# Building the operands of a feed-forward half inside attention instead of beside the output projection

## The chip, the cores and the metric

The kernel runs on one core of a Trainium2 chip. Its engines work side by side, each through its own instruction queue in order: TensorE (PE, matrix products and transposes, results in PSUM), VectorE (DVE), ScalarE (ACT), GpSimd (POOL) and SyncE (SP, which here only issues transfers). ACT also issues some transfers. The metric is device time in microseconds (us) of one execution; lower is better.

## The reference

One transformer block on 2048 tokens of width 576: a modulated layer norm, attention with 32 heads of 18 over four segments of 512 tokens with a running memory, an output projection with a gated residual, a second modulated layer norm, and a gated feed-forward network of width 4608 with its own gated residual.

```python
h = _layernorm(x) * (1 + ca) + sa
x = x + ga * _A_ref(h, A_wq, A_wk, A_wv, A_wo, A_beta)   # per segment: softmax + memory; then @ wo
h = _layernorm(x) * (1 + cb) + sb
x = x + gb * ((_silu(h @ w_gate) * (h @ w_up)) @ w_down)
```

All is float32. The kernel reaches that precision with products of split operands: a tile is rounded to a "high" part (a cast on ACT), and the rest, the "low" part, is formed by a subtraction on DVE; high x high, high x low and low x high are added in PSUM.

## The kernel before

**Attention** runs in 33 turns `u` of 11 steps `k`. Unit `u` is segment `s = u // 8` and group of four heads `q = u % 8`. In each step PE gets products of unit `u` (`p2_step`), the row maxima of unit `u + 2` (`p1_seq`) and events from a hand-written table `PAT`: the product with the values (`V`), its copy and transposes (`E`, `c`, `d`), the output projection of an earlier segment (`R`, `S`, `T`, `M`, `X`) and its layer norm, which stores the normalised tokens to DRAM (`xhD`). The event `n` stores a unit's row maxima to DRAM from ACT (`mD<-mr`, L211), and SP loads them back (`load_m`, `qs<-mD`, L174) for the first matmul of the next unit. At the start of each unit SP loads the stacks of a later one (`ks`, `qs`). Segment `s` is projected during the units of segment `s + 1`, so the last segment's projection stands alone behind attention.

**The feed-forward network** is done in two halves `t` of 1024 tokens. Each product of four blocks is formed by seven products of sums of blocks (a Strassen scheme). So each half needs seven operands `y[:, o]`, built from four blocks of normalised tokens, transposed and scaled: `h00`, `h10`, `h01`, `h11` (first index: which 512 tokens; second: which half of the columns). Operand 0 is `h00`, 1 is `h01`, 2 is `h11`, 3 is `tb = h10 - h00`, 4 is `tc = h11 - tb`, 5 is `cu = h11 - h10`, 6 is `h01 - tc`. Each comes in three column blocks `kb` (two of 128, one of 32 + 64 rows in which both parts stand together). The weights go through the same scheme: `load_o` loads a block of weights `O`, four `sum_o` on POOL add up its sums (L1091), `prep_r` and `prep_w` split them.

In the second half the operands are built during the first half (`prep2`), stored to DRAM (`yD`) and loaded (`load_y`). In the first half they are built by `t_prep` after attention, interleaved by the lists `TT` and `EE` with the last segment's projection (the seam): loads of `xhD` (L909, L912), transposes on PE (L918), scaling on ACT or DVE (L925, L922), differences on POOL and DVE (L946, L949, L953, L959), and 21 pairs of a cast (L932, L934) and a subtraction (L938, L940).

The projection itself: `wo_r` transposes, `wo_s` and `wo_t` split, `wo_m` issues the 14 matmuls of a block (L707; eight blocks, two PSUM banks), and `wo_x` (L712, DVE) adds the residual and so frees the bank. Work appended to `later` is issued on DVE at the next `flush`.

After the seam the loop over pairs of weight columns starts, 14 steps each; beside its products a pair issues `load_d`, `mul_d`, `sum_d` and `prep_d` for the second matrix (`dr`, L1108 to L1126). In the first pair the products with the second matrix (`pd`, L1257) are not there yet. The order on every engine is the order of the program.

Of the kernel before, what the change touches and what calls it, by code (L numbers as in the profile page):

```python
# [7 lines left out]
F32 = mybir.dt.float32  # L8
# [7 lines left out]
P = 128  # L16
# [29 lines left out]
T0 = 2  # L46
E0 = 4
EV = ((0, 0, 1), (0, 1, 0), (2, 1, 1))
EH = "aaap"
# [8 lines left out]
WC = 4  # L58
NE = 2
# [15 lines left out]
def block(ctx: ExitStack, tc: tile.TileContext, x, wqk, wv, wo, beta, wgu, wd, c, w_mod, out):  # L75
# [70 lines left out]
    yD = [dr.tile([P, 5, L], F32, tag=f"yD{o}", name=f"yD{o}") for o in range(7)]  # L146
# [511 lines left out]
    op = pool(p2r, "op", side="right")  # L658
    woh = w3.tile([P, 5, D], F32R, tag="woh", name="woh")
# [15 lines left out]

    def wo_r(s, i):
# [6 lines left out]
        xr = o3.tile([P, D], F32, tag="xr", name="xr")  # L683
        oT[s, i] = (oh, ol, xr)
        r = L * s + P * i
        nc.sync.dma_start(xr, x[r:r + P, :])
# [213 lines left out]
    def t_prep():  # L900
        xs, h = {}, {}

        def load(kb, kh):
            xt = xs[kb, kh] = xp.tile([P, 8, P], F32, tag="xs", name="xs")
            c0 = 288 * kh + 128 * kb
            for b in range(2):
                src = xhD[b][:, :, c0:c0 + min(P, 288 - 128 * kb)]
                if kb < 2:
                    nc.sync.dma_start(xt[:, 4 * b:4 * b + 4, :], src)  # L909
                else:  # L910
                    for j in range(3):
                        nc.sync.dma_start(xt[:, 4 * b:4 * b + 4, 32 * j:32 * j + 32], src)  # L912

        def trans(kb, kh, b):
            n = P if kb < 2 else 96
            pt = ps.tile([P, 4, P], F32, tag="t", name="pt", bufs=4)
            for i in range(4):
                nc.tensor.transpose(pt[:n, i, :], xs[kb, kh][:, 4 * b + i, :n], ident)  # L918
            h[kb, b, kh] = f = (hx if kb == 1 else tp).tile([P, L], F32, tag="sg", name="h", bufs=4 if kb == 1 else NSG)
            c = 3 * kh + kb  # L920
            if (kb, kh, b) in EV:
                nc.vector.tensor_scalar(f[:n], pt[:n].rearrange("p a b -> p (a b)"), colm[:n, c, 0:1], colm[:n, c, 1:2],  # L922
                                        op0=ALU.mult, op1=ALU.add)
            else:
                nc.scalar.activation(f[:n], pt[:n].rearrange("p a b -> p (a b)"), AF.Identity,  # L925
                                     scale=colm[:n, c, 0:1], bias=colm[:n, c, 1:2])

        def hi(kb, o, f, eng):
            n = P if kb < 2 else 96
            d = y[:n, o, kb if kb < 2 else 4]  # L930
            if eng == "a":
                nc.scalar.copy(d, f[:n])  # L932
            else:
                nc.gpsimd.tensor_scalar(d, f[:n], 1.0, 0.0, op0=ALU.mult, op1=ALU.add)  # L934

        def lo(kb, o, f):
            if kb < 2:
                nc.vector.tensor_tensor(y[:, o, 2 + kb], f, f32(y[:, o, kb]), op=ALU.subtract)  # L938
            else:
                nc.vector.tensor_tensor(y[64:96, o, 4], f[64:96], f32(y[64:96, o, 4]), op=ALU.subtract)  # L940

        def ew(kb):
            n = P if kb < 2 else 96
            t1, t2, t3, t4 = [tp.tile([P, L], F32, tag=g, name=g, bufs=2 if g == "cu" else 1) for g in ("tb", "tc", "cu", "cu")]
            h00, h10, h01, h11 = [h[kb, b, kh] for kh in range(2) for b in range(2)]
            nc.gpsimd.tensor_tensor(t1[:n], h10[:n], h00[:n], op=ALU.subtract)  # L946
            hi(kb, 0, h00, "a")
            yield
            nc.vector.tensor_tensor(t3[:n], h11[:n], h10[:n], op=ALU.subtract)  # L949
            lo(kb, 0, h00)  # L950
            hi(kb, 1, h01, "a")
            yield
            nc.gpsimd.tensor_tensor(t2[:n], h11[:n], t1[:n], op=ALU.subtract)  # L953
            lo(kb, 1, h01)
            hi(kb, 2, h11, "a")
            yield
            lo(kb, 2, h11)
            hi(kb, 5, t3, EH[0])
            nc.gpsimd.tensor_tensor(t4[:n], h01[:n], t2[:n], op=ALU.subtract)  # L959
            yield  # L960
            hi(kb, 3, t1, EH[1])
            lo(kb, 5, t3)
            yield
            hi(kb, 4, t2, EH[2])
            lo(kb, 3, t1)
            hi(kb, 6, t4, EH[3])
            yield
            lo(kb, 4, t2)
            lo(kb, 6, t4)
            yield  # L970

        def tr(kb):
            for kh in range(2):
                for b in range(2):
                    trans(kb, kh, b)
                    if b and kb < 2:
                        load(kb + 1, kh)
                    yield

        for kh in range(2):  # L980
            load(0, kh)
        return [tr(k) for k in range(3)], [ew(k) for k in range(3)]

    def prep2():
# [4 lines left out]
        def opr(kb, hv, o, f):  # L989
            n = P if kb < 2 else 96  # L990
            st = x2p.tile([P, 2, 256], F32R, tag="st", name="st", bufs=4)
            nc.scalar.copy(st[:n, 0], f)
            c = slice(256 * hv, 256 * hv + 256)
            yield
            if kb < 2:
                nc.vector.tensor_tensor(st[:, 1], f, f32(st[:, 0]), op=ALU.subtract)
                nc.sync.dma_start(yD[o][:, kb:kb + 3:2, c], f32(st))
            else:
                nc.vector.tensor_tensor(st[64:96, 0], f[64:96], f32(st[64:96, 0]), op=ALU.subtract)
                nc.sync.dma_start(yD[o][:96, 4, c], f32(st[:96, 0]))  # L1000
            yield
# [53 lines left out]
    def load_y(o):  # L1055
        nc.sync.dma_start(f32(y[:, o, 0:4]), yD[o][:, 0:4])
        nc.sync.dma_start(f32(y[0:96, o, 4]), yD[o][0:96, 4])
# [218 lines left out]
    with tc.manual_schedule():  # L1276
# [7 lines left out]
        for u in range(NU + 1):  # L1284
# [6 lines left out]
            for k in range(11):  # L1291
                next(ga, None)
                next(gb, None)
                for ev in PAT[q // 4 * 2 + u % 2][k].split():
                    event(ev, u)
            run(ga)
# [10 lines left out]
        wrp = pool(p4, "wrp", 2)  # L1307
        p5 = ExitStack()
        hx = pool(p5, "hx")
        tr, ew = t_prep()  # L1310
        for _ in range(T0):
            next(tr[0])
# [5 lines left out]
        run(tr[0])  # L1318
        ge = chain(*ew)
        for _ in range(E0):  # L1320
            next(ge)
# [3 lines left out]
        load_o(0, 0, 0)  # L1325
        load_o(0, 0, 1)
        gt, gw = chain(tr[1], tr[2]), iter(MP[:PF])
# [24 lines left out]
        run(ge)  # L1352
        for m in gw:
            prep_w(0, 0, m)
# [11 lines left out]
        for j in range(len(SS) - 4, 4):  # L1366
            sum_o(0, 1, j)
# [10 lines left out]
        for t in range(2):  # L1378
            for p in range(NPR):
                last = t == 1 and p == NPR - 1  # L1380
                nx = (p + 1) % NPR
# [9 lines left out]
                for k in range(14):  # L1391
# [14 lines left out]
                    if t == 0 and p == NPR - 1 and k in (7, 9, 10, 11, 12, 13) or t == 1 and p == 0 and k == 1:  # L1406
                        load_y(ACT_OP[m])
# [10 lines left out]
                    else:  # L1418
# [15 lines left out]
                        if k in (6, 7, 8, 9) and p < NPR - 2:  # L1434
                            sum_d(p, k - 6)
# [9 lines left out]
                        elif k == 12:  # L1445
                            nc.scalar.dma_start(wdD[p][:, :NS[p]], RW[p][:, :NS[p]])
                        elif k == 13 and tn == 0:
                            store_o(nx, 1)
                    if t and k == 2 + 2 * swap:
# [27 lines left out]
                    if is_plain(t, p):  # L1477
                        if k in (5, 6, 7, 10):
                            j = (5, 6, 7, 10).index(k)
# [74 lines left out]
```

## Time and profile before

| | us |
|---|---|
| median of 3 runs | 1931.91 |
| lowest and highest | 1925.47, 1933.14 |
| the profiled execution | 1926.12 |
| its span, first to last instruction | 1924.3 |
| PE, PEld, DVE, ACT, POOL busy | 1874.0, 1562.5, 1512.8, 929.8, 581.0 |
| mean granted TensorE clock | 0.996 |

All times of single instructions come from the one profiled execution, counted from its first instruction. A row of a timeline has the start, the duration, the engine (PEld is a weight load, SPq or ACTq a transfer being issued), the line of the kernel, the operation, and its output and inputs by name. Several equal instructions in a row share one line (x3), with the time from the first's start to the last's end. "[0.69 <-DMA qs<-mD]" says that the engine was idle for 0.69 us before it and what ended the wait. In the list of waits the three numbers are the total in us, the number of times and the longest. By the trace attention's last projection matmuls end at 615.23 us, and the first product of the feed-forward network starts at 656.04.

### The profile page before, as it was taken

What the parts mean: (1) busy time and instruction counts of PE and PEld (TensorE: products, weight loads), DVE (VectorE), ACT (ScalarE), POOL (GpSimd) and SP (SyncE); (2) the same over time, 40 slices, a digit from 0 to 9 for tenths busy, and PEclk for the clock granted to TensorE, in tenths of its full rate; (3) what the DMA queues carried; (4) which work ended last, traced back from release to release, by engine and by line L of the source; (5) the groups of instructions that cost most, each with busy time, mean ns of one, the idle gap of its engine ahead of it and who ended that gap; (6) DMA issues with size and microseconds to landing.
All of it is one profiled execution on the core that took longest, in us unless ns stands there. A gap on an engine that the chain in (4) does not pass through costs nothing.

```text
span 1924.3 us, 30622 instructions
## 1 busy us (share of the span) xinstructions
PE 1874.0 (97%) x10927; PEld 1562.5 (81%) x10927; DVE 1512.8 (79%) x3267; ACT 929.8 (48%) x2036; POOL 581.0 (30%) x772
## 2 busy tenths in 40 slices
PE   7999999999999799999999999999999999999999
PEld 4888865676766678888888888888888888888888
DVE  6575257878786888898898888776888888888887
ACT  2222257767666444445445444443544444454542
POOL 5222235555544554545444545410000000000000
PEclk9999999999999899999999999999999999999999
DMA  7777565444443555454454554478333233333331
GB/s 209 251 230 245 199 200 150 124 147 145 138 127 117 172 199 175 155 191 151 159 186 154 163 168 145 137 246 267 101 106 113 79 122 101 122 101 97 106 108 60
DMA packets 173543, 296.63 MB, mean 154 GB/s; under 512 B 25104, under 2 KB 101776, under 8 KB 171920
## 3 DMA queue, kind: packets, MB, share of 16 engines
q1 hardware_dynamic: 143280, 237.09, 39.4%
q10 hardware_dynamic: 30112, 57.60, 8.6%
q8 instruction: 86, 1.41, 0.3%
q14 instruction: 65, 0.53, 0.1%
HBM read 185.29 MB, written 109.31 MB: 153 GB/s over the span
## 4 chain that ended last, share of the span: by engine, by line
PE 88%; DMA 5%; DVE 4%; POOL 1%; issue 1%; ACT 1%; SPq 0%; ACTq 0%; POOLq 0%; DVEq 0%
PE A L1136 23%; PE pd L1257 13%; PE C L1136 12%; PE pd L1240 9%; PE B L1136 6%; PE s L589 4%; PE av L609 4%; PE pp L101 4%; PE s L187 4%; PE pv L101 3%; PE pw L707 2%; DMA y<-yD 1%; DMA mD<-mr 1%; PE pn L778 1%; DVE y L938 1%
## 5 line engine op out<-in xcount | busy, mean ns | idle before, releaser
L1136 PE MATMUL A<-y,wh 128*128 128x512 f32 x1152 | 406.8, 394 | 4.3 <-ACT B L1182 1.8
L192 DVE CUSTOM_DVE_ANT_0 junk<-s,tri 128x256 bf16<-128x256 f32 (+3 forms) x512 | 228.6, 487 | 75.6 <-PE s L187 67.6
L1101 DVE TENSOR_TENSOR wl<-O,wh 128x256 fp32r<-128x256 f32 x504 | 261.7, 525 | 4.2 <-ACT wh L1100 3.5
L1136 PEld LDWEIGHTS A<-y,wh 128*128 128x128 f32 x1152 | 217.2, 189 | 49.0 <-ACT B L1182 2.5
L592 ACT ACTIVATE Pt<-s 128x512 f32<-128x512 f32 (+1 forms) x352 | 186.6, 559 | 86.2 <-PE s L589 71.6
L1136 PE MATMUL A<-y,wl 128*128 128x512 f32 x576 | 227.2, 394 | 0.0
L1091 POOL TENSOR_TENSOR O<-O 128x384 f32<-128x384 f32 x144 | 163.3, 1146 | 179.1 <-DMA O<-in_wgu_dram 76.0
L1245 DVE TENSOR_TENSOR acc<-acc,pd 128x576 f32<-128x576 f32 x216 | 162.4, 752 | 58.6 <-PE pd L1240 51.7
L1136 PE MATMUL C<-y,wh 128*128 128x512 f32 x576 | 202.6, 392 | 1.0 <-DVE cu L1159 1.0
L1100 ACT CAST wh<-O 128x256 fp32r<-128x256 f32 x504 | 196.4, 405 | 1.9 <-POOL dr__8754 L1119 1.2
L1257 PE MATMUL pd<-dh,ah 128*128 128x288 f32 x640 | 189.1, 295 | 0.1
L1257 PE MATMUL pd<-dh,al 128*128 128x288 f32 x640 | 189.1, 295 | 0.0
L1257 PE MATMUL pd<-dl,ah 128*128 128x288 f32 x640 | 188.9, 295 | 0.0
L1261 DVE TENSOR_TENSOR acc<-acc,pd 128x576 f32<-128x576 f32 x156 | 116.9, 749 | 89.0 <-PE pd L1257 88.9
L1200 ACT CAST ah<-sg 128x512 fp32r<-128x512 f32 x192 | 119.1, 620 | 82.7 <-DVE sg L1160 77.6
L589 PE MATMUL s<-qs,ks 110*128 110x512 f32 (+2 forms) x384 | 149.2, 405 | 6.6 <-DMA qs<-mD 4.8
L187 PE MATMUL s<-ks,qs 108*128 108x256 f32 (+3 forms) x512 | 140.7, 326 | 2.9 <-DMA ks<-kD 1.4
L1201 DVE TENSOR_TENSOR al<-sg,ah 128x512 fp32r<-128x512 f32 x192 | 135.2, 704 | 8.8 <-ACT ah L1200 8.4
L1240 PE MATMUL pd<-dh,ah 128*128 128x288 f32 x448 | 133.0, 297 | 0.0
L1240 PE MATMUL pd<-dh,al 128*128 128x288 f32 x448 | 132.5, 296 | 0.0
L1240 PE MATMUL pd<-dl,ah 128*128 128x288 f32 x448 | 132.3, 295 | 0.0
L1257 PEld LDWEIGHTS pd<-dl,ah 128*128 128x128 f32 x640 | 120.5, 188 | 7.1
(349 smaller groups left out, 4394.4 us busy)
## 6 DMA issues: line engine op xcount, KB each, us to landing
O<-in_wgu_dram SPq DMA_DIRECT2D x36, 768.0 KB
oD<-O ACTq DMA_DIRECT2D x36, 512.0 KB
O<-oD SPq DMA_DIRECT2D x36, 512.0 KB
ks<-kD SPq DMA_DIRECT2D x68, 216.0 KB
qs<-qD SPq DMA_DIRECT2D x68, 216.0 KB
O<-in_wgu_dram SPq DMA_DIRECT2D x36, 384.0 KB
rD<-wr ACTq DMA_DIRECT2D x36, 336.0 KB
wr<-rD SPq DMA_DIRECT2D x35, 336.0 KB
```

The source lines that it names most:

```text
L187: nc.tensor.matmul(bank[:, n * (h - h0):n * (h - h0) + n], lhsT=qst[b][0:108, h, 128 * i:128 * i + 128], rhs=kst[b][0:108, h // 2, 0:n], s ...
L192: nc.vector.tensor_tensor_reduce(junk[:, :n], bank[:, n * (h - h0):n * (h - h0) + n], tri[:, L - n:], 1.0, -3e38, op0=ALU.add, op1=ALU.max ...
L589: nc.tensor.matmul(bank[:, n * (g - h):n * (g - h + w)].rearrange("p (a b) -> p a b", a=w), lhsT=kst[u % NB][0:110, g // 2, 128 * j:128 * ...
L592: nc.scalar.activation(pt[:, h:h + per, :n], bank[:, :n * per].rearrange("p (a b) -> p a b", a=per), AF.Exp, scale=SCALE)
L1091: nc.gpsimd.tensor_tensor(o[:, d], o[:, a], o[:, b], op=op)
L1100: nc.scalar.copy(wh, o)
L1101: later.append(lambda: nc.vector.tensor_tensor(wl, o, f32(wh), op=ALU.subtract))
L1136: nc.tensor.matmul(bank, lhsT=a, rhs=b, start=(first and n == 0), stop=(n == 6), skip_group_check=not first)
L1201: later.append(lambda: nc.vector.tensor_tensor(al, src, f32(ah), op=ALU.subtract))
L1240: nc.tensor.matmul(pd[:, i, :288], lhsT=a[:, tk], rhs=w, start=(k == 0), stop=(k == 2))
L1245: nc.vector.tensor_tensor(o, o, pd[:, :, :288], op=ALU.add)
L1257: nc.tensor.matmul(pd[:, i, :288], lhsT=a[:, tk], rhs=w, start=(k == 0), stop=(k == 5))
```

## The change

- The blocks of the first half are transposed during attention, one set of four transposes in each of units 18 to 29, at the step that `KP` gives, into the PSUM buffers `x` that attention uses. `stage_a` (units 18 to 23) takes the first 512 tokens: `h00` and `h01`, scaled by ACT into the new tile `yh`, split in halves of 256 columns, and both parts stored to DRAM (`yD[0]`, operands 0 and 1). `stage_b` (units 24 to 29) takes the second 512 tokens in pieces of 256: `h10` and `h11`; POOL forms operand 5 and `h10 - h00`, and operand 5 is split and stored. Loads are issued a unit ahead, stores some steps behind, all by SP. Staging buffers are tiles that are free by then (`mbd`, `pq`, `o1`).
- Beside the output projection only four operands are split: `y_sum` forms operands 4 and 6 on POOL (six subtractions), `y_here` splits operands 4, 3, 6, 2 in 12 casts and 12 subtractions, placed by `HH`. Operands 0, 1 and 5 are loaded from DRAM (`load_y`).
- The four tiles of `x` for the residual are loaded together ahead of the seam (`xr3`); the lists `SS` and `WW`, which place the sums and splits of the weights, change.
- In the first pair `mul_d`, `sum_d` and `prep_d` come two steps later (`dl`; `DK` lists the steps of the splits), the store of the second matrix one step later.
- `yD` has separate buffers for the two halves.

```diff
-TT = (0, 1, 2, 6, 12, 13, 14, 15)
-EE = (0, 1, 2, 7, 8, 8, 9, 10, 11, 12, 14, 16, 17, 18, 19, 22, 23, 27)
-WW = (19, 23, 25, 27, 30)
-SS = (2, 9, 11, 17, 18, 28, 29, 31)
+KP = (7, 8, 1, 3)
+WW = (9, 11, 14, 18, 26)
+SS = (2, 3, 4, 5, 18, 20, 22, 24)
+HH = (4, 6, 8, 10, 12, 13, 15, 17, 19, 21, 23, 25)
+DK = ((5, 6, 7, 10), (8, 9, 10, 11))
...
+    def y_part(g, o, kb, f, stf, hv, d=2):
...
+        def hi():
+            box.append(stf())
+            nc.scalar.copy(box[0][:n, 0], f[:n])
+        at(g, hi)
+        at(g + 1, lambda: y_lo(o, kb, f, box[0], c))
+        at(g + 1 + d, lambda: y_store(o, kb, box[0], c))
...
+    def step_of(u):
+        return 11 * u + KP[u % 8 // 4 * 2 + u % 2]
...
+    def stage_a():
...
+            at(11 * (u - 1) + 1 if i else 11 * u, lambda i=i, kh=kh, kb=kb: load_cols(xb[i % 2], 0, 0, kh, kb))
+            g = step_of(u)
+            at(g, lambda i=i, n=n: trans4(xb[i % 2], n, pts, i))
+            at(g + 1, lambda i=i, h=h, kh=kh, kb=kb: scaled(h, flat(pts.pop(i)), kh, kb))
+            for hv in range(2):
+                y_part(g + 2 + 3 * hv, kh, kb, h[:, 256 * hv:256 * hv + 256], lambda j=2 * i + hv: st[j % 3], hv)
...
+    def stage_b():
...
+            at(11 * (u - 1) + 1 if i else 11 * u, lambda i=i, hv=hv, kb=kb: load(i, hv, kb))
+            g = step_of(u)
...
+            at(g, trans)
+            at(g + 1, sc)
+            at(g + 2, lambda b=b, h11=h11, a=a, n=n: sub2(b[:n], h11, a[:n]))
+            at(g + 3, lambda h00=h00, a=a, n=n: sub2(h00, a[:n], h00))
+            y_part(g + 4, 5, kb, b, lambda i=i: sts[i % 2], hv)
...
                 for ev in PAT[q // 4 * 2 + u % 2][k].split():
                     event(ev, u)
+                for f in sched.pop(11 * u + k, ()):
+                    f()
...
-        tr, ew = t_prep()
-        for _ in range(T0):
-            next(tr[0])
+        xr3 = [load_xr(3, i) for i in range(4)]
...
+        load_o(0, 0, 0)
+        for j in range(3):
+            y_sum(j)
+        load_y(0, 0)
+        load_o(0, 0, 1)
+        load_y(0, 1)
+        load_y(0, 5)
         wo_z(3)
...
                     wo_m(3, i, h, c, 2)
-                    if n in TT:
-                        next(gt, None)
                     if c == 3:
                         wo_x(3, i, h)
-                    if n in EE:
-                        next(ge, None)
+                    flush()
                     if n in SS:
                         j = SS.index(n)
                         sum_o(0, j // 4, j % 4)
-                    if n == WW[0]:
-                        prep_r(0, 0, 0)
-                        prep_r(0, 0, 0, 1)
+                    if n in (7, 9, 11):
+                        y_sum(n // 2)
+                    if n in HH:
+                        y_here(HH.index(n))
                     if n in WW:
+                        j = WW.index(n)
+                        if j < 2:
+                            prep_r(0, 0, 0, j)
                         prep_w(0, 0, next(gw))
-                        flush()
...
+                dl = 2 if t == 0 and p == 0 else 0
...
-                        elif k in (4, 5):
-                            mul_d(p, k - 4)
+                        elif k - dl in (4, 5):
+                            mul_d(p, k - 4 - dl)
```

More of the change, by code (lines that the diff above doesn't have):

```diff
@@ L145, in block @@
     mD = [dr.tile([32, P], F32, tag=f"mD{b}", name=f"mD{b}") for b in range(NE + 4)]
-    yD = [dr.tile([P, 5, L], F32, tag=f"yD{o}", name=f"yD{o}") for o in range(7)]
+    yD = [[dr.tile([P, 5, L], F32, tag=f"yD{t}{o}", name=f"yD{t}{o}") for o in range(7)] for t in range(2)]
     xhD = [dr.tile([P, 4, D], F32, tag=f"xh{s}", name=f"xh{s}") for s in range(NSEG)]
@@ L682, in wo_r @@
         ol = o3.tile([P, 4, P], F32R, tag="ol", name="ol")
[L683 to L686, printed above, removed]
+        oT[s, i] = (oh, ol, load_xr(s, i) if s < 3 else xr3[i])
     def wo_s(s, i):
@@ L898, in block @@
     ACT_OP = {1: 0, 2: 1, 3: 2, 4: 6, 5: 3, 6: 4, 7: 5}
[L900 to L914, printed above, removed]
-            n = P if kb < 2 else 96
[L916 to L928, printed above, removed]
-            n = P if kb < 2 else 96
[L930 to L982, printed above, removed]
@@ new lines, in block, with at, y_lo, y_store @@
+    sched = {}
+    def at(g, f):
+        sched.setdefault(g, []).append(f)
+    def y_lo(o, kb, f, st, c):
+        if kb < 2:
+            nc.vector.tensor_tensor(st[:, 1], f, f32(st[:, 0]), op=ALU.subtract)
+        else:
+            nc.vector.tensor_tensor(st[64:96, 0], f[64:96], f32(st[64:96, 0]), op=ALU.subtract)
+    def y_store(o, kb, st, c):
+        if kb < 2:
+            nc.sync.dma_start(yD[0][o][:, kb:kb + 3:2, c], f32(st))
+        else:
+            nc.sync.dma_start(yD[0][o][:96, 4, c], f32(st[:96, 0]))
@@ new lines, in scaled, with trans4, flat @@
+    def scaled(dst, pt, kh, kb):
+        n, c = P if kb < 2 else 96, 3 * kh + kb
+        nc.scalar.activation(dst[:n], pt[:n], AF.Identity, scale=colm[:n, c, 0:1], bias=colm[:n, c, 1:2])
+    def trans4(xb, n, pts, key):
+        pts[key] = pt = ps.tile([P, 4, P], F32, tag="x", name="pt", bufs=XB)
+        for i in range(4):
+            nc.tensor.transpose(pt[:n, i, :], xb[:, i, :n], ident)
+    def step_of(u):
+        return 11 * u + KP[u % 8 // 4 * 2 + u % 2]
+    def flat(a):
+        return a.rearrange("p a b -> p (a b)")
@@ new lines, in stage_a @@
+    def stage_a():
+        sc = flat(yh[:, 2])
+        xb = [sc[:, L * i:L * i + L].rearrange("p (a b) -> p a b", b=P) for i in range(2)]
+        mb = mbd[:, 0:2].rearrange("p a b c -> p (a b c)")
+        st = [v.rearrange("p (a b) -> p a b", b=256).bitcast(F32R) for v in (sc[:, 2 * L:3 * L], mb[:, :L], mb[:, L:2 * L])]
+        pts = {}
+        for i in range(6):
+            kb, kh = divmod(i, 2)
+            u = 18 + i
+            n = P if kb < 2 else 96
+            h = yh[:, kh, kb]
+            at(11 * (u - 1) + 1 if i else 11 * u, lambda i=i, kh=kh, kb=kb: load_cols(xb[i % 2], 0, 0, kh, kb))
[4 more added lines that the diff above has]
+                y_part(g + 2 + 3 * hv, kh, kb, h[:, 256 * hv:256 * hv + 256], lambda j=2 * i + hv: st[j % 3], hv)
@@ new lines, in stage_b, with load, trans, sc @@
+    def stage_b():
+        big = flat(sk2.tile([P, 5, L], F32, tag="pq", name="yq"))
+        sts = [big[:, L * i:L * i + L].rearrange("p (a b) -> p a b", b=256).bitcast(F32R) for i in range(2)]
+        xb = [big[:, L * i:L * i + L].rearrange("p (a b) -> p a b", b=P) for i in (2, 3)]
+        sub = flat(opl_.tile([P, 4, D], F32, tag="o1", name="yo"))
+        h10 = [sub[:, 256 * i:256 * i + 256] for i in range(2)]
+        t3 = [sub[:, 256 * i:256 * i + 256] for i in (2, 3)]
+        pts = {}
+        def load(i, hv, kb):
+            for kh in range(2):
+                load_cols(xb[i % 2][:, 2 * kh:2 * kh + 2], 1, 2 * hv, kh, kb)
+        for i in range(6):
+            hv, kb = divmod(i, 3)
+            u = 24 + i
+            n = P if kb < 2 else 96
+            c = slice(256 * hv, 256 * hv + 256)
+            h00, h11 = yh[:n, 0, kb, c], yh[:n, 2, kb, c]
+            a, b = h10[i % 2], t3[i % 2]
+            at(11 * (u - 1) + 1 if i else 11 * u, lambda i=i, hv=hv, kb=kb: load(i, hv, kb))
+            g = step_of(u)
+            def trans(i=i, n=n):
+                trans4(xb[i % 2], n, pts, i)
+            def sc(i=i, kb=kb, a=a, c=c):
+                pt = flat(pts.pop(i))
+                scaled(a, pt[:, 0:256], 0, kb)
+                scaled(yh[:, 2, kb, c], pt[:, 256:512], 1, kb)
+            def sub2(d, x, y_):
+                nc.gpsimd.tensor_tensor(d, x, y_, op=ALU.subtract)
+            at(g, trans)
[3 more added lines that the diff above has]
+            y_part(g + 4, 5, kb, b, lambda i=i: sts[i % 2], hv)
@@ new lines, in y_sum, with y_here @@
+    def y_sum(j):
+        q, kb = divmod(j, 3)
+        n = P if kb < 2 else 96
+        t1, t4, h11, t2 = [v[:n] for v in (yh[:, 0, kb], yh[:, 1, kb], yh[:, 2, kb], ys[:, kb])]
+        if q == 0:
+            nc.gpsimd.tensor_tensor(t2, h11, t1, op=ALU.subtract)
+        else:
+            nc.gpsimd.tensor_tensor(t4, t4, t2, op=ALU.subtract)
+    def y_here(j):
+        o, kb = (4, 3, 6, 2)[j // 3], j % 3
+        n = P if kb < 2 else 96
+        f = ys[:, kb] if o == 4 else yh[:, (3, 6, 2).index(o), kb]
+        d = y[:, o, kb if kb < 2 else 4]
+        nc.scalar.copy(d[:n], f[:n])
+        if kb < 2:
+            later.append(lambda: nc.vector.tensor_tensor(y[:, o, 2 + kb], f, f32(d), op=ALU.subtract))
+        else:
+            later.append(lambda: nc.vector.tensor_tensor(d[64:96], f[64:96], f32(d[64:96]), op=ALU.subtract))
@@ L1293, in block @@
                 next(gb, None)
+                if u == 17 and k == 0:
+                    stage_a()
+                if u == 24 and k == 0:
+                    stage_b()
                 for ev in PAT[q // 4 * 2 + u % 2][k].split():
                     event(ev, u)
+                for f in sched.pop(11 * u + k, ()):
+                    f()
             run(ga)
@@ L1307, in block @@
         wrp = pool(p4, "wrp", 2)
+        xr3 = [load_xr(3, i) for i in range(4)]
         p5 = ExitStack()
-        hx = pool(p5, "hx")
-        tr, ew = t_prep()
-        for _ in range(T0):
-            next(tr[0])
+        ys = pool(p5, "ys").tile([P, 3, L], F32, tag="ys", name="ys")
+        load_o(0, 0, 0)
+        for j in range(3):
+            y_sum(j)
[3 more added lines that the diff above has]
+        load_y(0, 5)
         wo_z(3)
@@ L1317, in block @@
         wo_t(3, 0)
[L1318 to L1321, printed above, removed]
         wo_r(3, 1)
@@ L1324, in block @@
         wo_t(3, 1)
-        load_o(0, 0, 0)
-        load_o(0, 0, 1)
-        gt, gw = chain(tr[1], tr[2]), iter(MP[:PF])
+        gw = iter(MP[:PF])
         for i in range(4):
@@ L1351, in block @@
                     wo_t(3, i + 2)
-        run(ge)
-        for m in gw:
-            prep_w(0, 0, m)
         flush()
@@ L1365, in block @@
         g2 = prep2()
-        for j in range(len(SS) - 4, 4):
-            sum_o(0, 1, j)
         new_acc(accp, (2, 3, 4, 5))
@@ L1433, in block @@
                             sum_o(nx, 1, 2 * k - 19)
-                        if k in (6, 7, 8, 9) and p < NPR - 2:
-                            sum_d(p, k - 6)
+                        if k - dl in (6, 7, 8, 9) and p < NPR - 2:
+                            sum_d(p, k - 6 - dl)
                         if k == 0 and p == 0:
```

41 lines of the change are left out of this document (27 added, 14 removed).

## The prediction

> **What bounds the kernel now.** I read the chain of waits first: attention, then a broken stretch between 615 and 690 us, then unbroken TensorE (PE) products to the end. So I read busy time by stretch, with two of the attention units that get new work, one earlier unit, and the seam (the last projection, 615.2 to 656.0, and the first pair after it):
>
> ```profile
> 449.52:460.02 10.50, 10.50 (x78) 6.95 (x78) 8.93 (x40) 8.65 (x18) 5.83 (x11) 1.00 0.47 148
> 506.98:520.99 14.01, 14.01 (x105) 10.52 (x105) 10.93 (x46) 8.71 (x19) 6.34 (x15) 1.00 0.56 161
> 543.24:553.74 10.50, 10.50 (x78) 6.95 (x78) 8.94 (x40) 7.07 (x15) 4.67 (x10) 1.00 0.36 112
> 615.23:635.00 19.77, 14.80 (x113) 13.14 (x112) 18.70 (x22) 14.35 (x24) 13.23 (x11) 1.00 0.77 211
> 635.00:647.50 12.50, 7.12 (x53) 6.47 (x52) 12.41 (x14) 7.45 (x16) 11.72 (x10) 1.00 0.36 105
> 647.50:656.04 8.54, 4.84 (x22) 4.49 (x22) 8.29 (x14) 0.00 (x0) 1.57 (x2) 0.52 0.10 36
> 656.04:692.00 35.96, 31.40 (x127) 24.05 (x127) 26.69 (x42) 20.00 (x45) 18.22 (x15) 0.97 0.79 262
> ```
>
> The columns are the stretch, its length, busy time (and instructions) of PE, weight loads, VectorE (DVE), ScalarE (ACT) and GpSimd (POOL), granted clock, DMA share, GB/s. In attention PE is full. In the seam DVE is full (39.4 of 40.8 us), PE is not, and the clock falls to 0.52 at the end. The waits of 615 to 692 us confirm it:
>
> ```profile
> PE pw L707 <- DVE xr L712: 9.8, 4, 3.7
> POOL O L1091 <- DMA O<-in_wgu_dram: 7.2, 1, 7.2
> PEld pw L707 <- DVE xr L712: 5.6, 2, 4.1
> ACT dh L1125 <- POOL dr__8754 L1114: 2.2, 1, 2.2
> ```
>
> The projection's matmuls wait for a PSUM bank that `wo_x` (L712) must empty, and that is queued on DVE behind the splits of the operands (L938, L940). The timeline of DVE gives their price:
>
> ```profile
> 625.01 0.68 DVE L938 TENSOR_TENSOR y<-cu,y 128x512 fp32r<-128x512 f32 x1
> ...
> 630.32 4.85 DVE L938 TENSOR_TENSOR y<-h,y 128x512 fp32r<-128x512 f32 x3
> ...
> 645.71 0.46 DVE L712 TENSOR_TENSOR xr<-pw,xr 128x288 f32<-128x288 f32 x1
> ```
>
> With POOL idle a split takes 0.68; with POOL subtracting all the while, 4.85 / 3 = 1.62. The PSUM reader L712 stays at 0.46 beside POOL.
>
> **Seam: what goes and what stays.** Gone: 12 sets of four transposes (0.41 of PE each), their loads, evictions (three on DVE at 0.80), the difference `cu` on DVE (1.41, 1.65, 1.09) and 9 of 21 splits (operands 0, 1, 5). Staying on DVE with two SBUF inputs: 12 splits, 5 `wl`, 2 `wr`, about 10 us back to back; on POOL 6 subtractions of 1.28 and 8 `sum_o` of 1.01, 15.8 us. PE needs 8 blocks of 1.87 (14 matmuls, 0.133 apart) and its own transposes, some 17 us: its floor is 634.5 instead of 656.0. DVE and POOL keep it from there, so I walk the queues on the clock of before.
>
> SP: `xr3[1]` reuses a buffer whose store ACT issues at 615.92; I take 2.4 us to land (the small store of a maximum takes 1.4 in an idle queue). So the first weight load `O` goes out near 619, behind three loads of 0.29 MB. The two `O` loads of before, issued at 620.3, had moved by 627.6; here 624.5. POOL: three `y_sum` by 620.3, four `sum_o` 624.5 to 628.7, three `y_sum` at 1.65 to 633.7, four `sum_o` at 1.45 to 639.5. PE: blocks 0 to 3 and the transposes between, 618.7 to 627.0. ACT: at n = 11 the second part of `prep_r` needs all four `sum_o`, and everything behind it on ACT, three `y_here` casts among it, stops until 628.7. DVE then has `wr` 1.2, `wl` 0.9 and two splits of 1.6 ahead of the `wo_x` of block 3: 634.6, and only then block 5 starts. Another `wl`, `wo_t` and two splits beside POOL put the next at 639.2 (block 6), one more at 641.2 (block 7). The first pair starts at 643.0, against 656.04: **-13.0**. Bounds: -19 (637, since no `sum_o` can precede the load), and -5 (`O` two us later, half clock for three blocks).
>
> **First pair.** Its 13 steps and the 4 up to the first `pd` would take 17 x 1.61 = 27.4; they take 35.96. Delaying `mul_d` and `prep_d` by two steps takes away ACT's 2.2 for `dr`, behind which a copy held PE 1.0 at 674. POOL now does a `mul_d` (1.7) after the late load instead of in its idle time before, so it finishes about 1.7 later; the later splits have that slack or pay it. The first step, at half clock 2.7 instead of 1.6, gains 1.1 if the clock stays up. I take **-2.1**, bounds -4 and +3. Three operand loads (1.25 MB each) are issued by 622; at the 262 GB/s of the last row, all 6.5 MB from 618 are in by 643, and the first needed, operand 0, near 631. Nothing waits for them, but this cover is thin: operand 5 is used four steps in.
>
> **Attention.** PE gets the 12 sets: 12 x 0.41 = **+5.0**, all on the path, since PE is full there. ACT gets 0.78 + 2 x 0.41 = 1.6 a unit in 18 to 23 and about 1.3 in 24 to 29; DVE 0.84 and 0.42 (twice that beside POOL). Cover: the first and third row above are units with the same PE work, 8.65 and 7.07 of ACT, and the same 10.50. So 1.6 of ACT costs nothing up to there; most units end up at 8.4 to 10.3 of ACT in 10.9 to 14.4. Past it the price is bounded by one held-up step, 0 to 0.5 a unit; I take 0. POOL gets two half subtractions a unit in 24 to 29, covered by over 5 us idle.
>
> The queues: SP issues 1 load (3 to 6 for a third block) and up to 2 stores a unit, with `load_m` and the stack loads behind them. What that can delay is the row of maxima, stored by ACT, reloaded by SP, needed by the first matmul of the next unit. First unit 19, then 25:
>
> ```profile
> 473.64 0.31 ACTq L211 DMA_DIRECT2D mD<-mr  x1
> 477.86 0.23 SPq L174 DMA_DIRECT2D qs<-mD  x1
> 479.94 0.47 PE L589 MATMUL s<-qs,ks 110*128 110x512 f32 x1 [0.69 <-DMA qs<-mD]
> ```
> ```profile
> 555.67 0.31 ACTq L211 DMA_DIRECT2D mD<-mr  x1
> 557.07 0.23 SPq L174 DMA_DIRECT2D qs<-mD  x1
> ```
>
> Where loads are still draining, the store lands after 4.2 and PE waits 0.69; where they have drained, after 1.4, and nothing waits. By these rows 0.5 MB more in front (a load and a store, at the 161 GB/s of the second row 3.2 us) costs unit 20 up to 3.2 and units 21 and 22 up to 2.2 each (unit 21's row is reloaded at 489.15, lands 2.1 later as above, and is first used at 492.22, so 1.0 is spare): 0 to 7 together. I take 0 for the sum, as new pieces cover all 128 partitions and stack loads 108; 7 stays for the range. [...]
>
> **Sum.** -13.0 - 2.1 + 5.0 = -10.1 on the profiled execution's 1926.1 (span 1924.3): 1916.0. That execution lies 5.8 below the median of the runs shown, so on the median 1931.9 I say 1921.8, 0.52% less; 0.5% is about what a measurement of this kernel can tell from no change.
>
> **Rivals.**
> (a) The wait moves to POOL's sums: the gap before block 5 (627 to 634.6) lets the clock drop, as it did at 647.7 after gaps of 1.3 and 3.2 us (the 0.52 row). Three blocks and the first step at half speed, `O` at 626: start at 650.5, so -5.5, nothing saved in the first pair, +5.0: about 1931.4. For it: the same engines are queued in the same order. Against: fewer splits are left. It gets a quarter because the clock of before fell after shorter gaps. [...]
> (b) Slower: the row of maxima. If the new loads and stores hold it up by some 4.5 us in units 19 to 30 (the blocks of 128-byte pieces went at 79 GB/s in the seam), slacks of 0 to 2.7 are used up and each of 12 units starts late by 1.7 on average: +20. 1921.8 + 20 = 1942. It decides against the change from 1.7 a unit; for it unit 19, against it the idle DMA share (0.36) in units 24 to 29.
> (c) The seam falls to its bound, -19: 1915.8.
>
> **Chances.** Forecast with (c) 0.50, of which 0.40 beyond 0.5% faster and 0.10 within; (a) 0.25: 0.20 within, 0.02 faster, 0.03 slower; (b) 0.25: 0.23 slower, 0.02 within. Together 0.42, 0.32, 0.26. The forecast's own range is 1913 to 1930; 8 in 10 reaches to 1912 and, for (b), to 1942.
>
> **What would show it.** Right: no transposes of `xs` in the seam, the first product of the first pair 28 us after attention's last projection matmul, not 41; units 24 to 29 longer by 0.4 each; no first matmul of a unit waiting for `qs<-mD` over 0.7. Wrong: `L174` issued over 5 us after its store in most units; `Pt` or `s` waiting in units 18 to 23; `pw` waiting for `wo_x` as long as the 15.4 us now; clock under 0.9 in the last projection; the first pair waiting for `y<-yD`.

## The result and the profile after

| | before | after |
|---|---|---|
| median, 20 runs each (us) | 1928.82 | 1933.28 |
| lowest and highest | 1925.47, 1933.14 | 1929.19, 1936.01 |
| profiled execution, its span | 1926.12, 1924.3 | 1936.01, 1934.3 |
| attention, copy of unit 17's output to that of unit 29 (units 18 to 29) | 136.98 | 150.47 |
| seam, start of attention's last projection matmul (615.09 before, 632.28 after) to first product | 40.95 | 31.44 |
| first pair, to the first `pd` | 35.97 | 37.19 |

The ratio is 1.0021, interval 1.0013 to 1.0028: slower by 0.2%. That lies inside the widest range of the prediction (1912 to 1942) and outside the forecast's own (1913 to 1930), and the time went up where 0.52% less was forecast. The profiled executions differ by 10.0 us of span: +13.5 in attention, -9.5 in the seam, +1.2 in the first pair, +1.1 behind it, and +3.7 before unit 18, where no instruction differs. There the 14 profiled executions of this case differ among themselves: unit 18 starts anywhere from 459.2 to 464.4 us. So below I compare stretches and not spans. A stretch varies too: the profiled execution of the changed kernel is the slowest of its 20, and with the same code attention took 148.3 and 149.7 us in two later runs (e5 and e6), against 150.5 here.

Busy time by stretch, as before (units 17, 20, 22, 25; then seam in two parts; then first pair):

```profile
453.28:463.76 10.48, 10.48 (x78) 6.93 (x78) 8.92 (x40) 8.65 (x17) 5.80 (x11) 1.00 0.49 145
489.26:507.67 18.41, 16.52 (x109) 11.88 (x109) 12.53 (x50) 11.64 (x27) 6.36 (x13) 0.91 0.80 209
518.28:532.75 14.47, 14.47 (x109) 10.88 (x109) 12.67 (x48) 9.85 (x23) 6.82 (x15) 1.00 0.72 177
557.03:568.84 11.81, 11.55 (x84) 7.75 (x84) 9.85 (x43) 8.24 (x18) 6.07 (x12) 1.00 0.56 149
632.28:652.00 19.72, 13.98 (x93) 13.07 (x91) 12.24 (x17) 8.15 (x17) 12.30 (x11) 0.91 0.83 282
652.00:663.72 11.72, 7.75 (x43) 7.24 (x44) 11.53 (x17) 3.87 (x9) 6.56 (x5) 0.71 0.45 157
663.72:700.91 37.19, 32.05 (x129) 24.33 (x128) 26.29 (x42) 20.13 (x45) 16.19 (x15) 0.95 0.74 250
```

Unit 22 pays what was forecast: 14.47 against 14.01, PE still full. Unit 20 does not. Before, it took 14.02:

```profile
482.75:496.77 14.02, 14.02 (x105) 10.53 (x105) 10.66 (x45) 10.18 (x23) 6.06 (x13) 1.00 0.59 168
```

Now it takes 18.41, with PE idle for 1.9 and the clock at 0.91. So attention did not only get the transposes; it got waits. The timeline of unit 20 shows the dearest one:

```profile
488.92 0.39 SPq L915 DMA_DIRECT2D yD<-mbd  x1
...
492.14 0.31 ACTq L208 DMA_DIRECT2D mD<-mr  x1
...
497.39 0.25 SPq L171 DMA_DIRECT2D qs<-mD  x1
497.72 0.40 ACT L926 CAST mbd<-yh 128x256 fp32r<-128x256 f32 x1 [2.65 <-DMA yD<-mbd]
...
498.03 0.97 ACT L589 ACTIVATE Pt<-s 128x384 f32<-128x384 f32 x2
...
498.56 0.50 PE L586 MATMUL s<-qs,ks 110*128 110x512 f32 x1 [1.82 <-ACT Pt L589]
```

ACT's cast into a staging buffer waits 2.65 until the store that last read this buffer has landed. SP issued that store (0.26 MB) at 488.92 behind the unit's stack loads and a block load, and it lands 8.7 us later. In the rows the exponentials `Pt` start on ACT only behind the cast (498.03), and PE's next scores wait 1.82 for a PSUM bank that they must empty. The row of maxima (492.14 to 497.39, 5.25 us) is late too, but not last here. In e5 and e6, with the same code, PE waits 1.51 and 2.02 at this place.

The waits of 632 to 701 us, seam and first pair:

```profile
PE pw L709 <- DVE xr L714: 7.7, 3, 6.5
PEld pw L709 <- DVE xr L714: 6.9, 2, 6.7
...
POOL O L1139 <- DMA O<-in_wgu_dram: 6.8, 1, 6.8
...
PE C L1184 <- DVE cu L1207: 3.8, 1, 3.8
...
ACT dh L1173 <- POOL dr__8803 L1162: 3.0, 1, 3.0
```

PE's waits for `wo_x`, 9.8 in four pieces before, are now 7.7, of which 6.5 lie before block 5, the place that the prediction's walk named. The weight loads' waits, 5.6 before and 6.9 now, fall into the same gaps and are no time of their own. New is 3.8 of PE for `cu` in the first pair, and ACT's wait for `dr`, meant to go, grew from 2.2 to 3.0.

### The profile page after: what moved, and what is told of

Its sections match the earlier page's. It is cut to its first block, busy times and chain, and to the rows that moved or that the text cites. A ratio compares the mean times of both kernels' runs of the same rounds, so it can differ in the third digit from the quotient of the medians.

```text
span 1934.3 us, 30685 instructions
## 1 busy us (share of the span) xinstructions
PE 1879.5 (97%) x10927; PEld 1564.6 (81%) x10927; DVE 1508.3 (78%) x3270; ACT 934.0 (48%) x2057; POOL 578.6 (30%) x778
## 4 chain that ended last, share of the span: by engine, by line
PE 85%; DMA 6%; DVE 4%; ACT 1%; issue 1%; POOL 1%; SPq 1%; DVEq 0%; POOLq 0%; ACTq 0%
PE A L1184 23%; PE pd L1305 12%; PE C L1184 11%; PE pd L1288 9%; PE B L1184 6%; PE pp L98 4%; PE s L586 4%; PE av L606 3%; PE s L184 3%; PE pv L98 3%; PE pw L709 2%; DMA y<-yD 2%; DMA mD<-mr 1%; PE pn L780 1%; DMA wml<-in_w_mod_dram 1%
## 5 line engine op out<-in xcount | busy, mean ns | idle before, releaser
L1184 PEld LDWEIGHTS C<-y,wh 128*128 128x128 f32 x576 | 108.3, 188 | 24.4 <-DVE cu L1207 4.2
```

The costliest lines, as they stand in the source:

```text
L1184: nc.tensor.matmul(bank, lhsT=a, rhs=b, start=(first and n == 0), stop=(n == 6), skip_group_check=not first)
```

## The experiments

Ratios are to the kernel before, run on the same chip in the same session; stretches are from one profiled execution each.

### Attention: with nothing, with transposes, with casts, with stores

```diff
 e1    if u == 17 and k == 0:
-          stage_a()
-     if u == 24 and k == 0:
-          stage_b()
+          for j_ in range(9):
+              at(11 * (18 + j_) + 5, lambda j_=j_: nc.gpsimd.memset(yh[:, j_ // 3, j_ % 3], 0.5))
 e2 (y_part; stage_a and stage_b stay)
-    at(g, hi)
-    at(g + 1, lambda: y_lo(o, kb, f, box[0], c))
-    at(g + 1 + d, lambda: y_store(o, kb, box[0], c))
 e3
-    at(g + 1 + d, lambda: y_store(o, kb, box[0], c))
```

In e1 POOL only fills `yh` with a constant; e2 leaves out the casts, subtractions and stores, e3 the stores alone. In all three the operands 0, 1 and 5 are loaded from `xhD` instead of `yD`, in the same sizes.

> Leaves out all the new work in attention: the blocks are not transposed, yh holds a constant, and operands 0, 1 and 5 are loaded from other data of the same size. So it prices the seam and the first pair alone. In the profile of the changed kernel units 18 to 29 grew by 13.4 us, the seam (end of attention's last projection matmul to the first product) shrank by 9.5, the first pair grew by 1.2. If these parts do not act on each other: units 18 to 29 as before within 1, and 8 to 9 us less than before in all. If the seam's saving hangs on what attention leaves behind (rival): the seam shrinks by more than 11 here.

> Leaves out the casts, subtractions and stores of operands 0, 1 and 5 in attention; loads, transposes, scalings and POOL's differences stay. Theory 'stores' (their traffic and the reuse of their staging buffers make the price beyond the transposes): units 18 to 29 grow by 5 to 6. Theory 'engines' (ACT's and DVE's added work delays the softmax): 7 to 8. Theory 'loads' (the new loads delay the row of maxima): 10 or more.

> Leaves out only the 18 stores of operands 0, 1 and 5 in attention; casts and subtractions stay. Theory 'stores': units 18 to 29 grow by 6 to 7, and the total is 2 us under before. Theory 'engines': 11 to 13, as with the whole change.

| | ratio (interval) | attention | seam | pair |
|---|---|---|---|---|
| e1 | 0.995 (0.9935 to 0.9964) | 136.3 | 30.7 | 37.4 |
| e2 | 1.000 (0.9989 to 1.0011) | 145.1 | 31.0 | 37.4 |
| e3 | 1.0009 (0.9998 to 1.0019) | 146.4 | 31.7 | 38.0 |
| after | 1.0021 (1.0013 to 1.0028) | 150.5 | 31.4 | 37.2 |

Without work in attention the change is faster by 0.5%; all of that is given back there, and the seam (30.7 against 31.4) does not depend on it. From e1 to e2 attention grows by 8.8: PE's busy time by 5.2, the transposes, and its idle time by 3.6. A timeline of e2 has that idle time in four places:

```profile
464.77 0.44 PE L944 MATMUL pt<-ident,yh 128*128 128x128 f32 x2 [0.74 <-DMA yh<-xh]
...
481.69 0.47 PE L586 MATMUL s<-qs,ks 110*128 110x512 f32 x1 [1.60 <-DMA qs<-mD]
...
543.17 0.63 PE L666 MATMUL ptr<-ident,o 128*64 128x128 f32 x4 [1.12 <-ACT yh L939]
...
568.24 0.50 PE L586 MATMUL s<-qs,ks 110*128 110x512 f32 x1 [0.16 <-ACT Pt L589]
```

The first load, issued only in its own unit; the row of maxima behind the block loads; and in unit 24 a PSUM bank that the transposed block still holds when the older projection wants it. Casts add 1.3. Stores add 4.1 in these executions, most of it unit 20 and the half clock behind its wait (granted 0.50 from 500.5 to 502.5); measured against e5 and e6 they add 1.9 and 3.3, and by the ratios 0.12%, some 2.3 us. None of the expected theories holds alone: above the kernel before, e2 stands at 8.1, nearest to 'engines' by the number but with waits for loads and for a bank, and e3 at 9.4, between 'stores' and 'engines'.

### Where the stores and loads stand in the queues

```diff
 e4 (y_store)
-    nc.sync.dma_start(yD[0][o]...
+    nc.scalar.dma_start(yD[0][o]...
 e7 (both loads)
-    at(11 * (u - 1) + 1 if i else 11 * u, ...
+    at(11 * (u - 1) + 6 if i else 11 * u, ...
 e8 (step_of)
-    return 11 * u + KP[u % 8 // 4 * 2 + u % 2]
+    return 11 * u + {18: 9, 24: 6}.get(u, KP[u % 8 // 4 * 2 + u % 2])
```

> The same stores, issued by ACT and not by SP. If a store waits for SP's backlog only because it stands in SP's queue: it lands within 3 us, the 2.65 us wait of ACT for the staging buffer in unit 20 is gone, and units 18 to 29 grow by 8 to 9. If the DMA engines are the queue: the wait stays, and ACT's issue time (0.35 each) comes on top, 13 to 15.

Ratio 1.0023 (1.0014 to 1.0033), attention 148.9, between the two theories. The store that unit 20 waits for took 7.3 us to land instead of 8.7, and not under 3, so its place in SP's queue is only a small part of the delay. ACT waited 1.40 for it instead of 2.65, PE 0.68 for `Pt` instead of 1.82, and the unit took 15.77. That the store is the cause of unit 20's stall is shown by e3, where without it the unit took 14.78 and PE did not stall. Freed from SP's queue the store buys nothing that the whole run shows.

> Issues the loads of blocks at step 6 of the unit before, not at step 1. At step 1 they stand in front of the row of maxima (stored at step 2 to 4, loaded by SP after it). With the casts and stores left out, units 18 to 29 still grew by 8.1, of which 4.9 are transposes and 1.6 a wait for that row in unit 19. Theory 'backlog': the row lands within 3.5 us of its store instead of 4.2 to 6.3 and units 18 to 29 grow by 9 to 11 instead of 13.4. Rival 'engines': no change within 1.

Ratio 1.001 (1.000 to 1.002), attention 146.3, unit 20 15.06: with the load out of its way the store still took 7.9 us and ACT waited 0.82 for it, but PE no longer stalled behind that. Attention grew by 9.3, as the theory 'backlog' said, but not by its mechanism: the row of maxima still took 3.9 to 6.4 us in units 19 to 23. A later load now comes late in its turn:

```profile
485.55 0.65 PE L947 MATMUL pt<-ident,yh 128*128 128x128 f32 x4 [0.94 <-DMA yh<-xh]
```

> Moves the transposes of unit 18 from step 7 to 9 and of unit 24 from 7 to 6. In unit 18 PE waited 0.67 to 0.74 for the first load; in unit 24 the transposes of the projection waited 1.12 for the PSUM bank that the new transposes held until ACT had scaled them. If these two waits are real losses: units 18 and 24 are shorter by 0.7 and 1.1, 1.8 off the total. If the time comes back in the next unit: under 0.5.

Ratio 1.0027 (1.0016 to 1.0039), attention 150.1: of the 1.8 us expected the whole run shows nothing. Unit 18 lost its wait (11.98 against 12.72); unit 24, transposed a step earlier, waits for its load instead of the bank, and unit 20 is as before:

```profile
545.83 0.41 PE L947 MATMUL pt<-ident,yq 128*128 128x128 f32 x2 [1.80 <-DMA yq<-xh]
```

### The seam: when the first weights come

```diff
 e5
+    load_o(0, 0, 0)
     xr3 = [load_xr(3, i) for i in range(4)]
```

> Issues the first load of O ahead of the four loads of x, whose second one waits for a store that ACT issues at the end of attention. Theory 'sums' (the seam's length hangs on the moment when O lands, through the four sums on POOL, ACT's split of the rest and the queue on DVE): O lands 5 us or more earlier and the seam shrinks by 3 to 5 from 31.3. Rival 'DVE and POOL sum' (the work of the two engines sets the length whatever the order): under 1.

Ratio 1.0004 (0.999 to 1.0018). The load is out 2.1 us before attention's last projection matmul instead of 4.5 after it, the first four sums end at 9.9 instead of 16.7, and the seam is 27.6 instead of 31.4, as the theory 'sums' said. What is late next: PE waits for `wo_x` 5.2 in two pieces (longest 3.6), DVE is busy without a break, and the clock falls, as two stretches of e5 show:

```profile
646.00:650.00 4.00, 1.84 (x7) 1.85 (x8) 3.94 (x6) 0.00 (x0) 3.61 (x3) 0.56 1.01 336
650.00:654.00 4.00, 4.00 (x21) 4.00 (x21) 3.91 (x9) 0.00 (x0) 0.00 (x0) 0.59 0.29 111
```

### The first pair: the delay

```diff
 e6
-    dl = 2 if t == 0 and p == 0 else 0
+    dl = 0
```

> Undoes the delay of mul_d, sum_d and prep_d by two steps in the first pair (dl = 0). The first pair took 35.96 us before and 37.2 to 38.0 with the change, where -2.1 had been forecast. If the delay is the cause: 36 or less, 1 to 2 us off the total. If the pair is longer for another reason (its loads of weights beside the operand loads that are now in the queues): 37 and more, no change of the total.

Ratio 1.0012 (1.0001 to 1.0022); first pair 34.96 instead of 37.19. POOL's timeline, first of the changed kernel, then of e6:

```profile
676.37 2.10 POOL L1139 TENSOR_TENSOR O<-O 128x384 f32<-128x384 f32 x2 [17.74 <-DVE wl L1149]
678.43 1.44 POOL L1162 TENSOR_TENSOR dr__8803<-dr__8803,gbB 128x576 f32<-128x576 f32 x1
```
```profile
665.25 1.44 POOL L1162 TENSOR_TENSOR dr__8803<-dr__8803,gbB 128x576 f32<-128x576 f32 x1 [9.90 <-DMA dr__8803<-in_wd_dram]
```

Without the delay the first `mul_d` runs in POOL's idle time as soon as its data is in, 4.8 us after the first product. With it, it stands behind the sums of the next weights, 14.7 us after the first product, and everything from ACT's `dh` on follows: PE's wait for `cu` is 3.77 with the delay and 1.17 without. In all executions of the changed kernel with the delay the pair took 37.1 to 38.2, in all without it 34.9 to 35.4.

### The three moves together, and what is left

```diff
 e9: e5 + e6 + e7
 e10: e9, and step_of
-    return 11 * u + KP[u % 8 // 4 * 2 + u % 2]
+    return 11 * u + {18: 9, 24: 10}.get(u, KP[u % 8 // 4 * 2 + u % 2])
 e11: e9, and
-WW = (9, 11, 14, 18, 26)
+WW = (9, 14, 16, 20, 26)
```

> The changed kernel with the three moves together that were tried singly: the first pair's weights loaded ahead of the residual rows, no delay of two positions in the first pair, and the block loads of attention issued at step 6 instead of step 1 of the unit before. Theory 'the three places are independent': attention (copy of unit 17's output to that of unit 29) 146.5 us as with late loads alone, seam 27.6 as with the weights first, first pair 35.0 to 36.0 as without the delay; with the kernel before at 136.98, 40.95 and 35.97 that is 233.9 + ... = 209.6 us for the three stretches against 213.9, so 4.3 us under the kernel before, ratio 0.9978. By the three single medians (1928.9, 1929.15 and 1929.95 beside a kernel before of 1927.38, the changed kernel standing at 1.0021 of it) the gains add to 6.3 us off 1931.4: 1925.1, ratio 0.9988. Rival 'one wait takes the other's place' (the earlier seam meets the extracted weights for the output projection, and without the delay POOL's differences for the first pair meet the last sums): the first pair stays at 37 or more, or attention at 148 or more, and the ratio is 0.9995 to 1.001.

The "233.9 + ..." in this text is a slip; the sum of its three stretches is 146.5 + 27.6 + 35.5 = 209.6. Measured: ratio 0.9975 (0.9963 to 0.9987), attention 146.3, seam 30.1, pair 34.9. The moves add up, but for 2.5 us of the seam. Of these 1.5 are lost before the first wait for `wo_x`, and they go with the clock. PE waits for the first transposes, some 1.06 and 0.95 us, in e9, in e5 and in the changed kernel alike; in e9 and in the changed kernel some 3.5 us at half clock follow (0.24 us from one `pw` matmul to the next), in e5 none (0.13). So in these single executions the earlier load is worth 1.4 us where the clock falls there (30.1 against 31.4) and 3.7 where it does not (27.6 against 31.3 in e8).

> The three moves, and two sets of transposes moved within their units: unit 18's from step 7 to step 9, so that its load has landed, and unit 24's from step 7 to step 10, behind the last step's output projection piece, which had waited 1.12 us for the PSUM bank that the transposed blocks held. Theory 'unit 24's wait is the bank': no wait of a ptr or pto product on ACT yh at L942 in unit 24, none of over 0.3 us for the load in unit 18, and 1.5 us less than with the three moves alone in attention, 145.0; ratio 0.0008 under that of the three moves. Rival 'the wait moves on': unit 24 or 25 waits instead for the same bank, for the scaled block or for the exponentials behind ACT's scaling, attention 146 to 147, and the ratio is the same within 0.0004.

Ratio 0.9966 (0.9953 to 0.998), the fastest complete version, some 0.3% under the kernel before; its interval overlaps that of e9. Unit 24, first in e9, then in e10:

```profile
538.37:552.07 13.70, 12.57 (x96) 8.93 (x96) 10.36 (x41) 8.92 (x18) 6.78 (x13) 1.00 0.58 155
```
```profile
539.43:551.82 12.39, 12.39 (x96) 8.96 (x96) 10.27 (x41) 8.54 (x18) 6.57 (x13) 1.00 0.61 168
```

The bank's wait is gone and did not move on. Attention was still 147.4 in this execution and not 145.0, because of two other waits 2.7 us apart, behind which the clock was at half speed for some 6 us (granted 0.50, 0.50 and 0.56 from 486 to 492):

```profile
482.62 0.47 PE L586 MATMUL s<-qs,ks 110*128 110x512 f32 x1 [0.90 <-DMA qs<-mD]
485.31 1.11 PE L947 MATMUL pt<-ident,yh 128*128 128x128 f32 x4 [0.93 <-DMA yh<-xh]
```

The profiled execution of e12, the same code up to there, took 144.8.

> The three moves, with the preparation of the first pair's weights spread later beside the last output projection (its steps 9, 14, 16, 20 and 26 instead of 9, 11, 14, 18 and 26). Theory 'in the seam ACT and DVE are short in the middle of the output projection': with the weights early, that run showed the output projection waiting for the residual rows' extraction 1.6 and 3.6 us and a granted clock of 0.54 in the 6 us behind; moving the weight preparation away from there takes these waits to under 2 us in sum and the seam from 27.6 to 25 to 26, ratio 0.001 under that of the three moves. Rival 'the first product is set by the last weight preparation': the seam stays at 27.6 or grows by the shift, up to 29, and the ratio is the same or up to 0.001 higher.

Ratio 0.9986 (0.9977 to 0.9996), seam 28.9, waits for `wo_x` 6.0 in sum against 5.8 in e9. The theory is wrong: moving the weights' splits does not shorten these waits. The rival's number fits: among executions with full clock at the start of the seam, 28.9 stands against 27.6 (e5) and 27.9 (e10). That the last split of the weights sets the first product is not shown by it, as e9, with the lists of e5, took 30.1.

```diff
 e12: e10, and in y_here
+    if o in (4, 3):
+        return
 (ahead of wo_z(3))
+    for o in (4, 3):
+        nc.scalar.copy(y[:, o, 2:4], yh[:, 0, 0:2])
```

> The last version (three moves and two steps) with six of DVE's twelve subtractions for the four operands of the seam left out: operands 4 and 3 get their high part, but as low part two copies of a block made by ACT at the start of the seam, so these two operands are wrong. With the weights early, DVE was busy 3.9 us of every 4 between 638 and 654, and the two waits of the output projection for its bank, 1.54 and 3.60, lay behind such subtractions. Theory 'DVE's queue is what holds the seam now': the six take 7.1 us there; without them both waits go (under 1.5 us together), the clock stays at 1 and the seam falls from 27.9 to 22 to 24, ratio to the kernel before near 0.994. Rival 'POOL's sums of the weights hold it' (the split of the weights waits for them, and the last stands at step 26): the two waits become idle time of DVE, and the seam stays at 26 or more, ratio 0.996 to 0.997.

Ratio 0.9964 (0.9951 to 0.9976), seam 25.3: between both theories. PE's waits in the seam, from its timeline, and the clock of the first:

```profile
627.00 1.11 PE L684 MATMUL pto<-ident,o 128*128 128x128 f32 x4 [2.19 <-DVE or L673]
...
643.26 0.37 PE L709 MATMUL pw<-woh,oh 128*128 128x288 f32 x1 [0.96 <-ACT wh L1150]
645.75 0.40 PE L709 MATMUL pw<-woh,oh 128*128 128x288 f32 x1 [0.41 <-DVE xr L714]
```
```profile
626.00:630.00 4.00, 3.00 (x13) 3.00 (x14) 2.07 (x3) 2.33 (x5) 3.92 (x5) 0.50 0.67 212
```

The 1.54 and 3.60 for `wo_x` of e10 have shrunk to 0.41, so DVE's queue of subtractions is what held the seam there. But the two copies that stand in for them keep ACT from the transposed rows at the start: a wait of 2.19 where e10 has 0.95, then half clock (0.50 from 626 to 630) up to about 632. How short the seam gets without DVE's backlog is left open by this run.

## Why the prediction went wrong

**Attention, +5.0: the failed term.** Its PE part was right (5.2 of busy time in e2). Wrong was "Past it the price is bounded by one held-up step, 0 to 0.5 a unit; I take 0". Over twelve units that bound allows 6.0, PE's added idle time was 5.0, and unit 20 alone, with 1.9, broke it. ACT was counted as busy time against the length of a unit, and that was covered, as unit 22 shows. What was not walked is which of ACT's new instructions wait, and what is queued behind them. The casts wait for staging buffers, whose stores SP issues behind stack loads (1.82 in unit 20, then a granted 0.50: that unit's busy time is 1.5 above that of e5 and e6, the same code at full clock); a bank waits for ACT's scaling (1.12); the first block is loaded in the unit that uses it (0.67). Idle time of PE in units 18 to 29 went from 0.69 to 5.69 us; with 5.2 for transposes, 1.5 for the clock and 1.8 of other busy time, whose cause stays open, that makes the 13.5. The clock's part belongs to this execution: in e5 and e6 it stayed at 1.00 there, with 5.3 and 6.7 of idle time.

**The row of maxima, 0 taken of 0 to 7.** It was late as the bound said: over 4.8 us in five units (up to 6.3), where before only one was (5.0). In the changed kernel's profile something else came last, but the row came last for 1.60 in e2 and for 1.54 in e6, so 0 was too low. No run shows the reason given for 0, how many partitions the pieces cover. ACT issues this small store itself, and from it to the reload went 1.4 us at a DMA share of 0.07 (555.67 to 557.07 before), but 4.8 to 6.3 at shares of 0.44 to 0.81 in these five units. Rival (b) had the sign and the place near, but a price of 20 us for this row alone, which no run shows. The change also loses from less than the "1.7 a unit" named there: its forecast gain of 10.1 is used up at 0.84 in each of twelve units.

**Seam, -13.0: right mechanism, mis-sized term.** Counted from attention's last projection matmul, forecast against measured: `O` issued 3.8, 4.5; the first sum on POOL 9.3, 11.8; four sums done 13.5, 16.7; block 5 starts 19.4, 23.5; the first product 27.8, 31.4. The largest term is the landing of `O`: 5.5 us forecast, 7.3 measured. It had been read from a sum on POOL in the profile before (627.6) that waited for DVE and not for the load. The load also went out 0.7 later, the four sums took 0.7 longer, and the step from there to block 5 took 0.9 longer. e5, which only moves this load, gives 27.6. (The floor of 634.5 does not follow from its own 17 us, which end at 632.2; no term of the sum rests on it.) The part of rival (a) that the gap costs clock was right as well (0.71 in the second part of the seam), a price that the forecast had left out.

**First pair, -2.1: wrong sign.** The prediction wrote that later splits "have that slack or pay it" and took the slack. They paid: +1.2, and -1.0 without the delay (e6). That -1.0 is about the 1.1 forecast for the first step, whose clock was 0.75 before and is 1.00 in e6. No product waited for `y<-yD` there, so that cover held.

Of its tests, these spoke against it: `Pt` waiting in unit 20, clock under 0.9 in the seam, the first product at 31 and not 28, and units 24 to 29 longer by 0.9 on average and not 0.4. Its test of the waits for `wo_x` used 15.4, which counts the weight loads' waits a second time; by PE alone it is 7.7 against 9.8.

## What to carry to other kernels

Work moved under a full engine cost more here than its busy time (attention grew by 13.5 us, the transposes are 5.2 of them): walk every new instruction for what it waits on (a staging buffer's last store, a PSUM bank, a load) and name what stands behind it on its engine, since here a cast that waited 2.65 for a store held up the exponentials, and these the products by 1.82. Put the load that opens a stretch ahead of loads that can wait (here 1.4 to 3.7 us of the seam), and leave work in the idle time where it runs at no cost instead of delaying it behind a queue (here 2.2 us). A loss of 0.2% was here a gain of 0.5% and a new cost of 0.7%; three small moves, found from the waits, turned it into a gain of 0.25%, half of what e1 shows without the work in attention.

## What was not expected of the hardware

The granted clock fell after short pauses. In the changed kernel one idle gap of 1.82 us, with PE full before and after it, was followed by this:

```profile
494.00:496.00 2.00, 2.00 (x17) 1.96 (x16) 0.72 (x3) 1.07 (x2) 0.81 (x1) 1.00 0.71 231
496.00:498.50 2.50, 0.74 (x7) 0.52 (x5) 0.35 (x2) 0.78 (x3) 0.00 (x0) 1.00 0.17 55
498.50:500.50 2.00, 1.94 (x13) 1.78 (x17) 1.83 (x11) 2.00 (x6) 1.92 (x3) 0.69 0.84 221
500.50:502.50 2.00, 2.00 (x11) 0.76 (x12) 1.52 (x9) 0.34 (x1) 1.74 (x5) 0.50 1.03 368
```

Two gaps of 0.90 and 0.93 did the same in e10 (0.50 to 0.56 behind them). But behind one of 1.60 in e2, and one of 2.02 in e6 at the same place as the 1.82, it stayed at 1.00. At the start of the seam the same two waits (1.06 or 1.07, then 0.95) stand in 12 executions, and half clock followed them in 3: the changed kernel, e6 and e9 (0.24 us from one `pw` matmul to the next in the first and the last, 0.13 in e5 and e10). So on this record the length of a gap alone does not tell whether the clock falls. Second, a 0.26 MB store issued behind a unit's stack loads took 8.7 us to land, and in ACT's queue it still took 7.3 (e4), so the other queue did not free it.
